# A fused adaLN, long-convolution and shift-mixer kernel: input rows turned on TensorE, two swap buffers exchanged, the half block of the third layer split over two column groups, and about ninety single moves in a written-out order

## The chip, the core and the metric

The kernel runs on one core of a Trainium2 chip. The core has a matrix engine (TensorE, PE in the profile, with PEld for its weight loads), a vector engine (VectorE, DVE), an activation engine (ScalarE, ACT), a general engine (GpSimd, POOL) and a queue engine (SyncE, SP) that issues most of the DMAs. The metric is device microseconds of one execution. Lower is better.

## What is computed

All inputs are bf16. The sequence has S = 2048 rows of D = 640 channels; the hidden layer of the mixer has F = 1728.

```python
mod = (silu(c) @ w_mod)          # six vectors of 640: sa, ca, ga, sb, cb, gb
h = layernorm(x) * (1 + ca) + sa                 # x is A_q
k_shift = 4-tap causal filter of k along S, taps shift_k
kv = k_shift * v
y = causal long convolution of kv with ssm_k along S, by FFT of length 4096, + kv * ssm_D
x = x + ga * (h * y)
h = layernorm(x) * (1 + cb) + sb
u = gelu(layernorm(h) @ w1)                      # 640 x 640
u's four channel quarters are shifted along S by +1, -1, +2, -2 rows
x1 = h + u @ w2                                  # 640 x 640
h2 = gelu(layernorm(x1) @ w3) @ w4               # 640 x 1728, 1728 x 640
x = x + gb * (x1 + h2)
```

F is 13.5 blocks of 128, so w3 has a last block of only 64 columns, called the half block here.

## The kernel before, in words

**How the work is recorded and ordered.** Every piece of work is recorded by `add` as a task: an engine or a choice of engines, a closure that issues the instructions, and its reads and writes. Nothing is scheduled at run time. `ORDER` (line 26) is one string that lists all 1046 tasks by number, with the letter of the engine that is to run each (P, A, D, G for POOL, S for SP) and, after a colon, the places of the PSUM buffers that it takes (four of two banks each, 0 to 3). `Planner.run` checks that the string respects the dependencies, and then issues the tasks in that order. Each engine executes its own tasks strictly in this order. The `cost`, `rate` and `port` numbers of a task have no effect on this order. SP and POOL both issue DMAs, each through a queue of its own.

**The front (lines 224 to 387).** SP loads ssm_D as one column per channel block (line 224, `Dcol`, 640 elements of two bytes), the five blocks of the filter `ssm_k` (line 228, into Ra, 512 KB each), the shift taps (line 229, `skT`), the vector c (`c_col`) and, by transposing DMAs (line 233), k and v with channels on partitions. Meanwhile the twiddle tables of the FFT are made. POOL writes integer ramps (lines 287 and 302); `angles` multiplies and masks them on DVE (lines 292 and 293); `angles_pool` does the same in floating point with a rounding constant (lines 306, 308, 310), on POOL or DVE; ACT takes the sine (lines 316 and 321). F1bd is the table of the first FFT stage, Gs (in RG) that of the second, E (EA, EB, line 370) and H (via RK, copied into RH at line 576) those of the inverse. Of Gs a third is a negation (line 348), and six DMA copies spread it over partitions (lines 353 and 354). Line 355 makes the diagonal weights `diagw` of the shift filter out of `skT`. Lines 380 to 386 make silu(c) on POOL.

**The transforms.** Line 444 adds D to the filter's first sample, so that the skip path costs nothing later; `to_slots` (line 394) transposes 32x32 blocks on DVE; `stage1` (line 407) and `stage2_half` (line 427) are the two FFT stages on TensorE, evicted from PSUM by `evac` on ACT (line 207) or DVE (line 209). Stage one of the filter writes T01; half h = 0 is its lower half. `k_shift` (lines 463, 468) makes kv, which goes the same way. `inverse1` (lines 613, 617, 628, 629) multiplies the two spectra for ten blocks: for each block the filter's spectrum, with its two partition halves swapped, is copied by DMA into one of four swap buffers `KSY` (block i uses buffer i mod 4), one half issued on SP and one on POOL. `inverse2` (line 661) gives y, 16 row tiles of 128 rows.

**The layers.** `ln1_stats` takes the statistics of the first layer norm of a row tile, on DVE (two bn_stats and an aggregate, lines 539 and 540) or on ACT (two activations with an accumulator, lines 547 and 548). `chain_a`, `chain_b` and `chain_c` take groups of one or two tiles (`CG`) through the gating and two layer norms. `ln_finish` makes a norm's scale: the mean steps of lines 702 to 707 on POOL or DVE, then lines 712 to 717 on POOL, after the sum of squares from ACT (line 729). `turn` transposes a tile, on TensorE for early groups (line 772) and by a transposing DMA on SP for later ones (line 765). `mm_w1` (lines 818, 828), `mm_w2` (line 873), `mm_w3` (line 907, gelu at line 911) and `mm_w4` (lines 937 and 928) are the four layers; `mm_w2` and after work on the groups `MG`: seven pairs and the single tiles 1 and 0, tile 0 last. The result is stored by SP (lines 969 and 987).

**The half block.** Before, `w3_sb` is padded: a POOL copy (line 1020) repeats the last 64 columns behind themselves, so that the last block has 128 columns and its output holds the same 64 hidden channels on both partition halves. In `mm_w4` function `half` (line 928) uses that: for a pair, tile 0 takes its half block from partitions 0 to 63 and tile 1 from partitions 64 to 127, side by side.

## Time and profile before

| | |
|---|---|
| Runs | 301.48 us median of three (300.99 to 302.75) |
| The profiled execution | span 298.7 us from the first to the last instruction; what the runs' time holds beyond the span is 2.8 us by the median |
| PE | busy 269.7 us, 3176 matmuls |
| DVE, ACT, POOL | busy 218.2, 208.3 and 104.8 us |
| Granted TensorE clock | mean 0.975 of full speed |
| From 0 to 105 us | PE 90.6, DVE 101.1, ACT 93.6 us busy |
| From 105 to 140 us | PE 26.7, DVE 30.7, ACT 31.5 us busy, clock 0.84 |
| From 140 to 294 us | PE 152.4, DVE 85.6, ACT 83.2 us busy |
| DMA | 35.76 MB in 58356 packets, 40032 of them under 512 bytes |

A row of the profile names the source line, the engine, the operation, and output and input by the program's names with buffer numbers left out, so ps_w is any of the layers' PSUM tiles and R any tile called R with a number. A timeline row gives start and duration in us. In square brackets stand the idle time of that engine just before and what released it. A busy PE is modelled from its pipelined matmuls and overlaps a little from row to row; the chain of what ended last shows how far apart they really are.

### The profile page before, as it was taken

The page shows a single profiled execution, that of the slowest core. Times are in us where ns is not written, and L with a number is a line of the kernel's source. Part 1 is how long each engine was busy: PE and PEld are TensorE (multiplying, and loading weights), DVE is VectorE, ACT ScalarE, POOL GpSimd, SP SyncE. Part 2 cuts the span into 40 slices and gives each one's busy share as a digit, 9 for nine tenths or more (in the row PEclk, how much of TensorE's full clock was granted, in tenths as well). Part 3 has the DMA queues.
Part 4 walks back from the last instruction along what each step waited for, and adds up shares of the span by engine and source line. Part 5 has one row for each costly group of instructions (what it writes and reads, how often), then busy time and mean ns, then how long its engine had stood idle before and what let it go on. Part 6 is the DMA issues. An engine that isn't in the chain of part 4 may idle for free.

```text
span 298.7 us, 7890 instructions
## 1 busy us (share of the span) xinstructions
PE 269.7 (90%) x3176; PEld 208.5 (70%) x3182; DVE 218.2 (73%) x438; ACT 208.3 (70%) x341; POOL 104.8 (35%) x237
## 2 busy tenths in 40 slices
PE   0999999999989766869999999999999999999993
PEld 0666755777878436648878677787788767887871
DVE  8998999999999998898759589886361544212442
ACT  4799989999999789979868775766854705431200
POOL 5864364453216591434275426120421321100000
PEclk9999999999999859799999999999999999999999
DMA  6999999898999920563700203223113030510112
GB/s 215 275 215 184 225 137 246 225 217 221 229 253 281 280 65 2 153 203 69 273 4 0 46 5 68 56 46 60 41 40 80 5 89 6 63 43 23 29 52 60
DMA packets 58356, 35.76 MB, mean 120 GB/s; under 512 B 40032, under 2 KB 55008, under 8 KB 58320
## 3 DMA queue, kind: packets, MB, share of 16 engines
q1 hardware_dynamic: 57136, 32.01, 46.3%
q0 software_dynamic: 1088, 3.21, 4.1%
q8 instruction: 25, 0.41, 0.6%
q14 instruction: 11, 0.09, 0.1%
q10 hardware_dynamic: 96, 0.04, 0.1%
HBM read 16.31 MB, written 2.62 MB: 63 GB/s over the span
## 4 chain that ended last, share of the span: by engine, by line
PE 51%; DVE 13%; ACT 11%; DMA 10%; POOL 6%; issue 5%; SPq 2%; DVEq 0%; POOLq 0%; ACTq 0%
PE ps_w L937 17%; PE ps_w L907 14%; ACT T L207 5%; DMA Ra<-in_A_q_dram 5%; PE ps_w L873 4%; PE ps_w L818 3%; PE ps_s L427 3%; ACT RG L729 3%; DVE Rb L617 3%; PE ps_ksh L463 2%; POOL lnv L715 2%; PE ps_s L407 2%; DMA RK<-R 2%; DVE R L756 2%; PE ps_mod L493 2%
## 5 line engine op out<-in xcount | busy, mean ns | idle before, releaser
L907 PE MATMUL ps_w<-R,T 128*128 128x256 bf16 (+1 forms) x630 | 63.8, 261 | 0.7 <-DMA R<-RH 0.7
L907 PEld LDWEIGHTS <-T 128*128 128x128 bf16 x630 | 55.5, 98 | 7.9 <-issue 2.0
L937 PE MATMUL ps_w<-T,R 128*128 128x320 bf16 x416 | 59.1, 299 | 0.0
L911 ACT ACTIVATE R<-ps_w 128x1024 bf16<-128x1024 f32 (+2 forms) x36 | 28.8, 827 | 41.9 <-PE ps_w L907 41.9
L937 PEld LDWEIGHTS <-R 128*128 128x128 bf16 x416 | 40.5, 98 | 15.2
L960 DVE TENSOR_TENSOR T<-ps_w,R 128x640 bf16<-128x640 f32 x15 | 12.3, 822 | 35.4 <-PE ps_w L928 18.1
L207 ACT CAST T<-ps_s 128x1024 bf16<-128x1024 f32 x32 | 30.4, 1029 | 3.2 <-PE ps_s L407 3.1
L207 ACT CAST R<-ps_s 128x960 bf16<-128x960 f32 (+1 forms) x35 | 30.8, 964 | 1.8 <-PE ps_s L427 1.6
L407 PE MATMUL ps_s<-F1bd,Rb 128*128 128x256 bf16 x160 | 23.3, 298 | 8.7 <-DVE Rb L394 8.1
L729 ACT ACTIVATE RG<-R 128x640 bf16<-128x640 bf16 x32 | 23.5, 734 | 9.9 <-DVE R L880 6.7
L407 PEld LDWEIGHTS <-Rb 128*128 128x128 bf16 x160 | 16.7, 107 | 14.7 <-DVE Rb L394 8.6
L873 PE MATMUL ps_w<-RG,R 128*128 128x320 bf16 x160 | 23.2, 299 | 2.1 <-ACT R L820 2.1
L715 POOL TENSOR_TENSOR lnv<-lnv,mhalf 128x2 f32<-128x2 f32 (+1 forms) x29 | 22.5, 775 | 2.3
L427 PE MATMUL ps_s<-T,RG 64*128 64x160 bf16 x512 | 21.2, 230 | 0.8 <-ACT R L207 0.6
L880 DVE SCALAR_TENSOR_TENSOR R<-ps_w,R 128x640 bf16<-128x640 f32 x16 | 12.9, 819 | 11.8 <-PE ps_w L873 11.6
L427 PEld LDWEIGHTS <-RG 64*128 64x128 bf16 x512 | 17.7, 94 | 5.1 <-issue 4.6
L818 PE MATMUL ps_w<-R,RG 128*128 128x256 bf16 (+1 forms) x200 | 20.0, 259 | 1.3 <-DMA R<-RK 0.6
L873 PEld LDWEIGHTS <-R 128*128 128x128 bf16 x160 | 15.4, 98 | 8.2 <-ACT R L820 2.4
L629 PE MATMUL ps_i<-EB,Rb 128*128 128x128 bf16 x160 | 19.0, 219 | 1.5 <-DVE Rb L617 1.4
L818 PEld LDWEIGHTS <-RG 128*128 128x128 bf16 x200 | 17.1, 102 | 3.5 <-issue 2.0
L628 PE MATMUL ps_i<-EA,Rb 128*128 128x128 bf16 x160 | 19.0, 219 | 0.4 <-ACT R L207 0.3
L714 POOL TENSOR_TENSOR lnv<-stat,lnv 128x2 f32<-128x2 f32 x19 | 4.0, 212 | 40.9 <-ACT RG L729 28.7
(178 smaller groups left out, 513.5 us busy)
## 6 DMA issues: line engine op xcount, KB each, us to landing
Ra<-in_A_ssm_k_dram SPq DMA_DIRECT2D x5, 512.0 KB, 5.7
R<-in_w_mod_dram SPq DMA_DIRECT2D x6, 400.0 KB, 6.0
out_dram<-RH SPq DMA_DIRECT2D x60, 40.0 KB, 1.6
T<-in_B_w_dram SPq DMA_DIRECT2D x5, 432.0 KB, 6.2
RH<-in_w_mod_dram SPq DMA_DIRECT2D x4, 400.0 KB, 4.4
Ra<-in_A_q_dram SPq DMA_DIRECT2D x4, 320.0 KB, 6.6
RK<-R SPq DMA_DIRECT2D x5, 256.0 KB, 4.5
RK<-R POOLq DMA_DIRECT2D x5, 256.0 KB, 5.3
```

The source lines that it names most:

```text
L207: nc.scalar.copy(dst, src(ps.tile))
L407: nc.tensor.matmul(psv[:, ml, :], lhsT=xL[:, s0:s0 + P], rhs=F1r, start=True, stop=True)
L427: nc.tensor.matmul(psv[:, g, j], lhsT=Gs[p, k, 64 - 64 * cc:192 - 64 * cc], rhs=T1h[h][p, cc * 32 + k], start=(cc == 0), stop=(cc == 1), t ...
L628: nc.tensor.matmul(psv[:, w, :], lhsT=Av[:, r_, :, g_], rhs=EAf, start=True, stop=False)
L629: nc.tensor.matmul(psv[:, w, :], lhsT=Bv[:, r_, :, g_], rhs=EBf, start=False, stop=True)
L715: nc.gpsimd.tensor_tensor(rs, rs, mhalf[:, 0:n], ALU.pow)
L729: add("ACT", 0.74, lambda e: nc.scalar.activation(junk, src, ACT.Square, scale=float(D) ** -0.5, accum_out=stat[:, li, 1, t:t + 1]), r=[sk ...
L818: nc.tensor.matmul(pt[:, fb, 0:cw], lhsT=w1_sb[:, b, 160 * fb:160 * fb + P], rhs=hT[:, b, 0:cw], start=(b == 0), stop=(b == ND - 1))
L873: nc.tensor.matmul(pt[:, hf, 0:320], lhsT=gsf[:, fb, c0:c0 + P], rhs=w2_sb[:, fb, 320 * hf:320 * hf + 320], start=(fb == 0), stop=(fb == 4))
L907: nc.tensor.matmul(pt[:, fl, 0:cw], lhsT=w3_sb[:, b, fb * P:(fb + 1) * P], rhs=xT[:, b, 0:cw], start=(b == 0), stop=(b == ND - 1))
L911: nc.scalar.activation(g3[g % 2][:, f0:f0 + fn, 0:cw], ps.tile[:, 0:fn, 0:cw], ACT.Gelu_apprx_tanh)
L937: nc.tensor.matmul(bank(i, hf), lhsT=gg[:, fb, i * P:(i + 1) * P], rhs=w4_sb[:, fb, 320 * hf:320 * hf + 320], start=(fb == 0 and i == 0), ...
```

## The change

Five things are changed, and the order string is new as a whole because the tasks have new numbers (1054 of them now).

- **Rows turned on TensorE.** ssm_D, c and shift_k are loaded as contiguous rows of five partitions into T01 (free until the first FFT stage writes it). A 5x5 identity `eye`, made by POOL, and one matmul (for D) and five matmuls (for c and the four taps) turn them into columns, which ACT copies out of PSUM into `Dcol` and `csk`. `diagw` is laid out tap first. In the order SP issues one block of ssm_k first, then the D row, two blocks, the rows of the taps and of c, then the last two blocks.
- **Table front.** An early sine on ACT of a constant comes first. The small per-partition constants are split: nine one-column steps stay on DVE, six go to POOL. The two multiplications of the first Gs table (line 292) go from DVE to ACT, and its negation from DVE to ACT. The second Gs table has its scaling for both offsets on POOL and the two steps after the second one on DVE, where they were on DVE and POOL, and its negation moves from POOL to DVE. All five additions of D are on DVE (three were on POOL). The six copies of Gs are issued by POOL instead of SP.
- **Swap buffers.** In `KSY` the third and fourth entries are exchanged: the third block now uses the end of Rb and the fourth the upper half of RK, which holds the H table until its copies into RH are done. The order of the two blocks' copies on SP and POOL is exchanged too.
- **Half block.** `mm_w3` computes the half block with ten matmuls, 64 weight columns by 128 rows each, on two column groups of the array: for a pair, tile 0 on output partitions 0 to 63 and tile 1 on 64 to 127; for a single tile the same tile on both. The gelu of a pair then reads 384 columns instead of 512 in that task. The POOL copy of line 1020 is gone, and `half` reads its operand at columns 0 to 127 for both halves.
- **Moves.** The order of the PE tasks stays but for nine that move by one to four places. On ACT and DVE about fifty tasks stand elsewhere or change sides: the statistics of row tiles 14 and 10 go from DVE to ACT, several normalisations and turned tiles change between the two, and the mean steps of `ln_finish` for tiles 7 and 8 (second norm) and 9 and 10 (first norm) go from POOL to DVE. On SP the transposing copy of the second tile of the mixer group of tiles 8 and 9 moves ahead of that of the first and of three stores, and a few stores swap places. 156 of 223 PSUM tasks have another place.

```diff
-    diagw = RQ[:, 0:2560].rearrange("p (b j m) -> p b j m", b=ND, j=4)
+    diagw = RQ[:, 0:2560].rearrange("p (j b m) -> p b j m", b=ND, j=4)
...
-    KSY = [(RG[:, 6144:8192], ("RG", 6144, 8192)), (RK[:, 0:2048], ("RK", 0, 2048)), (RK[:, 2048:4096], ("RK", 2048, 4096)), (Rb[:, 8192:10240], ("Rb", 8192, 10240))]
+    KSY = [(RG[:, 6144:8192], ("RG", 6144, 8192)), (RK[:, 0:2048], ("RK", 0, 2048)), (Rb[:, 8192:10240], ("Rb", 8192, 10240)), (RK[:, 2048:4096], ("RK", 2048, 4096))]
...
-
-    def ld_tiny(q, dst, src):
-        with nc.allow_non_contiguous_dma(reason="tiny"):
-            q.dma_start(dst, src)
-
-    dma("SP", 8, lambda q: ld_tiny(q, Dcol[:], A_ssm_D.rearrange("(b p) -> p b", p=P)), w=[("Dcol", 0, 1)], rate=8.0)
+    csk = mem.tile([P, 5 * ND], BF, name="csk")
+    c_col, skT = csk[:, 0:ND], csk[:, ND:5 * ND].rearrange("p (j b) -> p b j", j=4)
+    rowD, rowc, rows = T01[0:ND, 0:P], T01[0:ND, P:2 * P], T01[0:ND, 2 * P:6 * P]
+
+    dma("SP", 8, lambda q: q.dma_start(rowD, A_ssm_D.rearrange("(b p) -> b p", p=P)), w=[("T01", 0, P)])
...
-    dma("SP", 8, lambda q: q.dma_start(skT[:], A_shift_k.rearrange("(b p) j -> p b j", p=P)), w=[("skT", 0, 1)], rate=30.0)
-    dma("SP", 8, lambda q: ld_tiny(q, c_col[:], c.rearrange("o (b p) -> p (o b)", p=P)), w=[("ccol", 0, 1)], rate=12.0)
+    dma("SP", 8, lambda q: q.dma_start(rows, A_shift_k.rearrange("(b p) j -> b (p j)", p=P)), w=[("T01", 2 * P, 6 * P)])
+    dma("SP", 8, lambda q: q.dma_start(rowc, c.rearrange("o (b p) -> (o b) p", p=P)), w=[("T01", P, 2 * P)])
...
+    one, eye = T01[:, 6 * P + 16:6 * P + 17], T01[:, 6 * P:6 * P + ND]
...
+        nc.vector.memset(one, 1.0)
...
-    add("DVE", 0.35, f, w=[("consts", 0, 1), ("kTp", 0, 1)])
+    add("DVE", 0.35, f, w=[("consts", 0, 1), ("kTp", 0, 1), ("T01", 6 * P + 16, 6 * P + 17)])
...
+        nc.vector.tensor_single_scalar(pci[:, 1:2], pidx[:], 63, ALU.bitwise_and)
+        nc.vector.tensor_single_scalar(pci[:, 2:3], pidx[:], 64, ALU.bitwise_and)
...
-        nc.vector.tensor_single_scalar(pci[:, 1:2], pidx[:], 63, ALU.bitwise_and)
+        nc.vector.tensor_single_scalar(pci[:, 3:4], pidx[:], 96, ALU.bitwise_and)
+        nc.vector.tensor_copy(s64[:], pci[:, 1:2])
+        nc.vector.tensor_copy(offi[:], pci[:, 2:4])
...
-        nc.vector.tensor_scalar(s32o[:], pci[:, 0:1], 2.0, 1.0, ALU.mult, ALU.add)
-        nc.vector.tensor_copy(s64[:], pci[:, 1:2])
-        nc.vector.tensor_scalar_mul(s32o[:], s32o[:], 1.0 / 8192)
-        nc.vector.tensor_scalar_mul(s64t[:], s64[:], 1.0 / 8192)
-
-        nc.vector.tensor_single_scalar(pci[:, 0:1], pidx[:], 64, ALU.bitwise_and)
-        nc.vector.tensor_single_scalar(pci[:, 1:2], pidx[:], 96, ALU.bitwise_and)
-        nc.vector.tensor_copy(offi[:], pci[:])
...
-        nc.vector.tensor_scalar(offc[:, 2:3], offi[:, 0:1], s64t[:], 0.5, ALU.mult, ALU.mult)
-        nc.vector.tensor_scalar(offc[:, 4:5], offi[:, 1:2], s32o[:], 0.5, ALU.mult, ALU.mult)
...
-        nc.vector.tensor_scalar_add(offc[:, 3:4], offc[:, 2:3], 0.25)
-        nc.vector.tensor_scalar_add(offc[:, 5:6], offc[:, 4:5], 0.25)
-    add("DVE", 1.9, f, r=[("pidx", 0, 1)], w=[("scol", 0, 1)])
+    add("DVE", 1.3, f, r=[("pidx", 0, 1)], w=[("scol", 0, 1)])
+
+    def f(e):
+        nc.gpsimd.tensor_scalar(s64t[:], s64[:], 1.0 / 8192, None, ALU.mult)
+        nc.gpsimd.tensor_scalar(offc[:, 2:3], offi[:, 0:1], s64t[:], 0.5, ALU.mult, ALU.mult)
+        nc.gpsimd.tensor_scalar(offc[:, 3:4], offc[:, 2:3], 0.25, None, ALU.add)
+        nc.gpsimd.tensor_scalar(s32o[:], s32[:], 2.0 / 8192, 1.0 / 8192, ALU.mult, ALU.add)
+        nc.gpsimd.tensor_scalar(offc[:, 4:5], offi[:, 1:2], s32o[:], 0.5, ALU.mult, ALU.mult)
+        nc.gpsimd.tensor_scalar(offc[:, 5:6], offc[:, 4:5], 0.25, None, ALU.add)
+    add("POOL", 1.0, f, r=[("scol", 0, 1)], w=[("scolt", 0, 1)])
+
+    add("POOL", 0.2, lambda e: nc.gpsimd.affine_select(out=eye, in_=one.to_broadcast([P, ND]), pattern=[[-1, ND]],
+                                                       compare_op=ALU.is_equal, fill=0.0, base=0, channel_multiplier=1),
+        r=[("consts", 0, 1), ("T01", 6 * P + 16, 6 * P + 17)], w=[("T01", 6 * P, 6 * P + ND)])
+    psD, psC = Slot(), Slot()
+
+    def f(e):
+        pt = pst(psD, name="ps_row")
+        nc.tensor.matmul(pt[:, 0, 0:ND], lhsT=rowD, rhs=eye[0:ND, :], start=True, stop=True)
+    add("ACT", 0.1, lambda e: nc.scalar.activation(lnv[:, 2, 0:1], b_pos[:], ACT.Sin), r=[("consts", 0, 1)], w=[("lnsp", 0, 1)])
+    t0 = add("PE", 0.1, f, r=[("T01", 0, P), ("T01", 6 * P, 6 * P + ND)], alloc=psD, ni=2)
+    t1 = add("ACT", 0.2, lambda e: nc.scalar.copy(Dcol[:], psD.tile[:, 0, 0:ND]), w=[("Dcol", 0, 1)], use=psD)
+
+    def f(e):
+        pt = pst(psC, name="ps_row")
+        nc.tensor.matmul(pt[:, 0, 0:ND], lhsT=rowc, rhs=eye[0:ND, :], start=True, stop=True)
+        for j in range(4):
+            nc.tensor.matmul(pt[:, 0, ND + ND * j:2 * ND + ND * j], lhsT=rows.rearrange("b (p j) -> b j p", j=4)[:, j, :], rhs=eye[0:ND, :], start=True, stop=True)
+    t0 = add("PE", 0.5, f, r=[("T01", P, 6 * P), ("T01", 6 * P, 6 * P + ND)], alloc=psC, ni=10)
+    t1 = add("ACT", 0.2, lambda e: nc.scalar.copy(csk[:], psC.tile[:, 0, 0:5 * ND]), w=[("ccol", 0, 1), ("skT", 0, 1)], use=psC)
...
-    def angles(reg, o, n, pattern, base, s_col, q, offs=None):
+    def angles(reg, o, n, pattern, base, s_col, q, offs=None, split=False):
...
-                nc.vector.tensor_scalar(m_, ti, s_col, off, ALU.mult, ALU.add)
+                if not split:
+                    nc.vector.tensor_scalar(m_, ti, s_col, off, ALU.mult, ALU.add)
...
+            if split:
+                add("ACT", 0.25 + 0.00095 * n, lambda e, m_=m_, off=off: nc.scalar.activation(m_, ti, ACT.Identity, scale=s_col, bias=off),
+                    r=[keys[0], ("scol", 0, 1)], w=[k_])
...
-                r=[keys[0], ("scol", 0, 1)], w=[keys[1]], port=0.5)
+                r=[keys[0], ("scol", 0, 1), ("scolt", 0, 1)], w=[keys[1]], port=0.5)
...
-            ms, ma, ky = angles("R3", o, 512, pat, base, s64[:], 8192, (offc[:, 0:1], offc[:, 1:2]))
+            ms, ma, ky = angles("R3", o, 512, pat, base, s64[:], 8192, (offc[:, 0:1], offc[:, 1:2]), True)
...
-        add(("POOL", "DVE"), {"POOL": 1.48, "DVE": 0.35}, lambda e, k2s=k2s: eng_of[e].tensor_scalar(Gs[:, k2s, 128:192], Gs[:, k2s, 0:64], -1.0, None, ALU.mult),
-            r=[wk[:3]], w=[wk], port=0.4)
+        def f(e, k2s=k2s):
+            if e == "ACT":
+                nc.scalar.mul(Gs[:, k2s, 128:192], Gs[:, k2s, 0:64], -1.0)
+            else:
+                eng_of[e].tensor_scalar(Gs[:, k2s, 128:192], Gs[:, k2s, 0:64], -1.0, None, ALU.mult)
+        add(("POOL", "DVE", "ACT"), {"POOL": 1.48, "DVE": 0.35, "ACT": 0.65}, f, r=[wk[:3]], w=[wk], port=0.4)
...
-        in_=skT[:].rearrange("p b j -> p (b j)").unsqueeze(2).to_broadcast([P, 4 * ND, P]),
+        in_=csk[:, ND:5 * ND].unsqueeze(2).to_broadcast([P, 4 * ND, P]),
...
+                    if fb == NF - 1:
+                        for b in range(ND):
+                            for i in range(2):
+                                c0 = P * i if cw > P else 0
+                                nc.tensor.matmul(pt[64 * i:64 * i + 64, fl, 0:P], lhsT=w3_sb[:, b, fb * P:fb * P + 64], rhs=xT[:, b, c0:c0 + P],
+                                                 start=(b == 0), stop=(b == ND - 1), tile_position=(0, 64 * i))
+                        continue
...
-                nc.scalar.activation(g3[g % 2][:, f0:f0 + fn, 0:cw], ps.tile[:, 0:fn, 0:cw], ACT.Gelu_apprx_tanh)
+                if cw > P and f0 + fn == NF:
+                    n = cw * (fn - 1) + P
+                    gf = g3[g % 2].rearrange("p f n -> p (f n)")
+                    nc.scalar.activation(gf[:, f0 * cw:f0 * cw + n], ps.tile[:].rearrange("p f n -> p (f n)")[:, 0:n], ACT.Gelu_apprx_tanh)
+                else:
+                    nc.scalar.activation(g3[g % 2][:, f0:f0 + fn, 0:cw], ps.tile[:, 0:fn, 0:cw], ACT.Gelu_apprx_tanh)
...
-            nc.tensor.matmul(bank(i, hf), lhsT=gg[p, NF - 1, i * P:(i + 1) * P], rhs=w4_sb[p, NF - 1, 320 * hf:320 * hf + 320],
+            nc.tensor.matmul(bank(i, hf), lhsT=gg[p, NF - 1, 0:P], rhs=w4_sb[p, NF - 1, 320 * hf:320 * hf + 320],
...
-    def f(e):
-
-        nc.gpsimd.tensor_copy(w3_sb[:, :, F:FP], w3_sb[:, :, F - 64:F])
-    add("POOL", 0.6, f, w=[("T01", 0, ND * FP)])
...

```

## What I predict, before seeing a run of it

> **What bounds the kernel now.** I read first the ten-microsecond windows (columns: PE, weight loads, DVE, ACT, POOL busy us with instruction counts, granted clock, DMA share, GB/s), since the average (PE 90%, DVE 73%, ACT 70%) mixes stages.
>
> ```profile
> 0.00:10.00 10.00, 1.88 (x9) 1.35 (x10) 8.84 (x32) 3.96 (x6) 6.60 (x16) 1.00 0.74 249
> ...
> 70.00:80.00 10.00, 9.29 (x181) 8.44 (x180) 9.87 (x11) 9.98 (x13) 2.05 (x4) 1.00 0.93 230
> ...
> 110.00:120.00 10.00, 7.63 (x168) 6.41 (x169) 8.95 (x24) 9.07 (x19) 3.13 (x17) 0.84 0.01 2
> ...
> 130.00:140.00 10.00, 7.25 (x95) 6.07 (x95) 8.43 (x24) 8.54 (x18) 3.94 (x11) 1.00 0.32 80
> ...
> 220.00:230.00 10.00, 10.00 (x91) 8.66 (x89) 3.79 (x11) 3.91 (x9) 2.64 (x9) 1.00 0.19 39
> ```
>
> There are three stages. Up to about 105 us DVE and ACT are full (the transforms; PE only follows their evictions). From 105 to 140 a chain through DVE, ACT and POOL (the layer norms) sets the pace and PE waits. From 140 to 294 PE is full, so only TensorE time or a PE wait counts. Behind it lie 4 us of last stores.
>
> Second, the timeline of the start (start, duration, idle before and its releaser):
>
> ```profile
> 0.80 0.46 SPq L224 DMA_DIRECT2D Dcol<-in_A_ssm_D_dram  x1
> ...
> 1.32 1.92 SPq L228 DMA_DIRECT2D Ra<-in_A_ssm_k_dram  x4
> ...
> 5.54 0.44 POOL L444 TENSOR_TENSOR Ra<-Ra,Dcol 128x1 bf16<-128x1 bf16 x1 [1.82 <-DMA Ra<-in_A_ssm_k_dram]
> ...
> 6.01 3.96 DVE L394 STREAM_TRANSPOSE Rb<-Ra 128x1024 int32<-128x1024 int32 x2
> ...
> 8.12 6.95 PE L407 MATMUL ps_s<-F1bd,Rb 128*128 128x256 bf16 x36 [8.12 <-DVE Rb L394]
> ...
> 9.19 2.84 ACT L207 CAST T<-ps_s 128x1024 bf16<-128x1024 f32 x3 [1.89 <-PE ps_s L407]
> ```
>
> DVE waits for the first filter block, ACT for PE: ACT is idle 6.0 of its first 9.19 us. Third, the timelines of the middle and of PE, where PE waits:
>
> ```profile
> 128.77 0.88 DVE L539 BATCH_NORM_STATS2 ln_st<-Ra 128x6 f32<-128x320 bf16 x2
> ...
> 129.69 0.21 DVE L540 BATCH_NORM_AGGREGATE mv<-ln_st 128x2 f32<-128x12 f32 x1
> ...
> 131.82 1.53 PE L873 MATMUL ps_w<-RG,R 128*128 128x320 bf16 x10 [2.08 <-ACT R L820]
> ...
> 170.72 2.34 PE L818 MATMUL ps_w<-R,RG 128*128 128x256 bf16 x20 [0.60 <-DMA R<-RK]
> ...
> 206.59 3.65 PE L907 MATMUL ps_w<-R,T 128*128 128x256 bf16 x32 [0.65 <-DMA R<-RH]
> ```
>
> After 141 us these last two are the only PE waits left: 1.25 us.
>
> **The front.** Before, the load of D in 640 two-byte pieces is queued first: the DMA view of the first 6 us shows 1 GB/s from about 1.9 us and the full 400 only from 3.5, so the first block lands at 5.40. After, that block is issued first, at 0.80. First bytes came 1.15 us after the first issue, 512 KB at 400 GB/s are 1.3, and some 0.6 passed from the last byte to the landing: 3.85. The D row, issued 0.46 later, comes at about 4.3; a matmul (0.3, as L407's), a copy of 5 columns (estimate 0.25, just under the 0.265 of the 32x128 activation) and the add on DVE (0.17) put the first transpose at about 5.2 instead of 6.01: 0.8 earlier, and PE and ACT with it.
>
> DVE then carries more: two 512-column steps of the second angle set come from POOL (L306 on DVE took 0.57, so 1.14) and two more adds (0.34); one L306 (0.57) goes to POOL; one negation (0.74) goes to ACT and the other comes from POOL. Net +0.9, which eats its 0.8. What leaves DVE ahead of the transposes (two multiplies of 0.54 and about six one-column steps) only ends in waiting for D. ACT gains 0.8 at the start and its 0.52 wait for POOL (L310) at 17.8, and pays one 25-column copy (0.25): -1.1. The two multiplies (0.65 each, as L316), the negation and the D copy fit its 6 us of idle time; the sine table load (1.28) starts at 0.79 either way. In a stage in which both engines are full I take the mean of about 0 and -1.1: **-0.5**. Bounds: -1.6 (the other 1280 tiny pieces, for the shift kernel and c, no longer sit between the transposing loads, and DVE's 0.38 and 0.51 us waits near 26 and 29 us go as well) and +1.5 (below).
>
> Covers. The shift and c rows share T01 with the first stage, so its h=0 evictions and everything behind five row matmuls on PE wait for them. Behind three blocks they land near 1.95 + 3x1.3 + 0.6 = 6.5; PE gets there at about 8.1: cover 1.6. If they take the 6.6 us of the old shift load (issue 3.2, landing 9.8), PE, ACT and DVE lose about 1.6. The six RG copies leave SP, which then starts the loads behind them sooner, for POOL: 6x0.5 of POOL time, and two POOL waits for landings. A copy from POOL landed in 5.3 us against 4.5 from SP (RK<-R). Behind them on POOL stand E, the H angles and the silu chain, which ended at 47.6 and is used at 54.0: 6.4 us of cover. The second stage (25.79) has only about 1 us; with the negation at about 19.5 the first copies land near 26: 0 to +1.5. I take 0, as PE is not the bound there.
>
> **Exchanged swap buffers.** The third and fourth exchange trade RK's upper half for Rb. The chain passes through those copies (67.4 to 76.1), but DVE, which uses them, is busy 9.87 of 10 between 70 and 80 us: 0, bounds -0.5 and +0.5.
>
> **The half block.** Seven pair groups spend five 256-column matmuls on it: the chain has 70 in 7.64, so 109 ns each, 0.55 per group. Two single groups spend 5x61 ns = 0.30 (20 of 128 columns in 1.22). After, ten matmuls of 64 columns of weights by 128, two at a time. No row shows two column halves; the nearest two:
>
> ```profile
> 254.78 0.45 PE L928 MATMUL ps_w<-T,R 64*128 64x320 bf16 x4
> ...
> 113.39 1.21 PE L661 MATMUL ps_i<-T,RH 32*32 32x160 bf16 x96
> 113.39 1.00 PEld L661 LDWEIGHTS <-RH 32*32 32x32 bf16 x96
> ```
>
> At the 136 ns of a 320-column matmul (26 in 3.53) a column is 0.425 ns. L928 (two row halves) takes 0.38 in the chain: two rounds of 136 ns, and 0.11 for the change of shape. The trace thus gives 5x54 + 110 = 0.38: -0.17 x7, +0.08 x2. The skill speaks against it. "TensorE: Matmul & The Clock Gate" (Part 3, What overlaps and what doesn't) lets a weight load overlap running matmuls only in another row group, and here both halves use all rows; its section on LDWEIGHTS gives columns/1.2 ns, 53 for 64, and "TensorEngine Tiling (Array Packing)" (Restrictions and Gotchas) rules out the fast load with column tiling. In series that is 10x(53+56) + 110 = 1.2 us: an estimate from these pages, +0.65 x7 and +0.9 x2, +6.4. But L661 uses four column and four row groups and loads 32 columns every 10.4 ns, where the rule gives 27, and 24 matmuls of 68 ns (160 columns) on one row group alone would fill 1.6 us, not 1.21. Column groups do overlap here, so I take the trace: -1.2 + 0.2 = **-1.0**, ends -2.0 (no change of shape) and +6.4. ACT saves 128 columns per pair (0.1), beside a full PE: 0. The POOL copy that filled the padding (0.45 at 135.49) goes; PE was busy with L873 then: 0.
>
> **The moves.** (a) The statistics of row tile 14 (L539, L540: 1.1 us) leave DVE at 128.8, where the chain passes through them, for ACT (two passes, 1.9), and some normalisations change sides. DVE's chain shortens by 1.1; ACT, busy 8.5 of 10, pays part back: **-0.8**, ends -2 (the whole 2.08 wait at 131.8) and +1.4 (ACT's net added work between 110 and 140, if ACT becomes last there). (b) The statistics of tile 10 (1.1 us at 156.8) leave the DVE chain that ends in the wait at 170.7, but ACT gets 1.9 and one normalisation (0.9) just ahead of the sums that POOL awaits next, and has about 1.7 of slack there: **-0.3**, ends -0.6 and +1.0. The mean steps that go from POOL to DVE ended 1.1 us before those sums: 0. (c) Of the pair of transposing copies (L765) that PE awaits at 206.6 the second was issued at 203.88, behind three stores (1.5 us on SP), and now goes ahead of them; it then lands by about 205, and PE comes at 205.9: **-0.6**, ends -0.65 and 0, and the stores have time. The other moves swap neighbours on engines with room: 0, ends -0.5 and +0.5.
>
> **Sum.** -0.5 - 1.0 - 0.8 - 0.3 - 0.6 = -3.2 on a span of 298.7, so 295.5. The median of the runs, 301.48, is 2.8 above the profiled span, taken as constant: **298.3**.
>
> **Rivals.** *Nothing but the half block*: the front ends in the same DVE work, and the middle is bound by ACT, which gets 1.4 us more. For: DVE's net +0.9, ACT above 9 of 10 from 110 to 130. Against: its 6 idle us at the start. 301.48 - 1.0 = 300.5; chance 0.17. *The front is worth more*: DMA is saturated from 4 to 34 us and 1920 tiny pieces go; the end -1.6, all of the 2.08 and 1.25 us waits, and -1.0: 301.5 - 5.9 = 295.6; chance 0.17. *Column halves run in series* (the slower side): 6.4 us on the full PE against 2.2 of gains elsewhere, 305.7. It passes +1.5 when the ten matmuls take over 0.9 us: nine groups then cost 8.1 against 4.4 before, +3.7 less the 2.2. L661 speaks against it; with smaller such losses (late rows, a stage-two stall) chance 0.11. The forecast itself, 296.5 to 299.9: 0.55.
>
> A measurement of this kernel can tell about 0.5%, 1.5 us, from no change. Faster 0.55 + 0.17 = 0.72, same 0.17, slower 0.11. The range leaves out the top (column halves in series) and a little below: 294.8 to 301.8.
>
> **What would show it.** First transpose near 5.2 and first eviction near 8.4; no PE wait at the five row matmuls; PE beginning its full stretch about 1.3 us earlier; ten L907 half matmuls within about 0.4 us; no waits at the two copies. It would be wrong if the halves take over 0.55 us, if stage two waits for RG, or if ACT is what PE awaits near 130.

## The result and the profile after

The changed kernel takes **306.22 us** (median of 14 runs, 302.32 to 307.80) against 301.81 (300.62 to 304.91) for the kernel before on the same chip: ratio **1.0112 [1.0088, 1.0136]**. This ratio, like all ratios with an interval here, leaves out runs over 1.5% above their kernel's own fastest; since kernels with copies on POOL spread widely, the ratio of the plain medians (here 1.0146) is given too. The forecast was 298.3 with a range up to 301.8, so it was wrong in sign. The profiled execution has a span of 304.1 (before 298.7) and itself took 305.98.

The windows of after, with the columns of the prediction's first fence:

```profile
0.00:10.00 10.00, 2.61 (x16) 1.60 (x17) 7.41 (x25) 6.52 (x13) 8.60 (x22) 1.00 0.75 257
10.00:20.00 10.00, 7.57 (x36) 4.54 (x35) 9.54 (x10) 7.12 (x8) 4.69 (x5) 1.00 1.16 222
...
30.00:40.00 10.00, 8.56 (x173) 6.51 (x175) 7.60 (x8) 7.65 (x9) 6.71 (x11) 1.00 1.28 195
...
70.00:80.00 10.00, 9.64 (x187) 8.03 (x187) 9.77 (x12) 9.78 (x13) 4.22 (x9) 1.00 0.86 232
...
110.00:120.00 10.00, 6.40 (x125) 3.88 (x124) 9.55 (x28) 8.97 (x19) 7.68 (x22) 0.53 0.27 61
...
130.00:140.00 10.00, 8.31 (x58) 5.74 (x59) 8.29 (x25) 9.33 (x21) 4.94 (x11) 0.83 0.64 211
...
220.00:230.00 10.00, 10.00 (x91) 7.57 (x90) 6.40 (x16) 5.11 (x10) 2.66 (x9) 1.00 0.18 39
```

The early windows are the ones to read. ACT is busy 6.52 of the first ten (before 3.96), as foretold. But from 30 to 40 DVE and ACT are down to 7.60 and 7.65, where before they had 9.50 and 9.49: in the stage in which both should be full, both wait. The DMA share is above 1 from 10 to 50 us. Before, in this window, and a mark that both kernels have, the first matmul into ps_mod, in before and in after:

```profile
30.00:40.00 10.00, 9.63 (x181) 7.02 (x177) 9.50 (x13) 9.49 (x12) 2.70 (x2) 1.00 1.17 207
...
54.04 0.84 PE L493 MATMUL ps_mod<-RH,silu_w 128*128 128x320 bf16 x5
...
59.70 0.84 PE L527 MATMUL ps_mod<-RH,silu_w 128*128 128x320 bf16 x5
```

The mark comes 5.7 us late, which is as much as the whole loss (span +5.4). By PE's rows the loss is complete even earlier: the eight stage-one matmuls that begin at 41.35 in before begin at 46.94 in after. What follows gives a little back.

The timeline of the start of after (start, duration, idle before and its releaser) answers the second fence:

```profile
4.79 2.07 DVE L428 STREAM_TRANSPOSE Rb<-Ra 128x1024 int32<-128x1024 int32 x1
...
6.91 1.89 PE L441 MATMUL ps_s<-F1bd,Rb 128*128 128x256 bf16 x8 [2.56 <-DVE Rb L428]
...
7.98 1.02 ACT L208 CAST T<-ps_s 128x1024 bf16<-128x1024 f32 x1 [1.25 <-PE ps_s L441]
...
9.46 0.18 PE L300 MATMUL ps_row<-T 5*128 5x5 bf16 x1 [0.67 <-DMA T<-in_c_dram]
...
10.37 3.23 DVE L478 TENSOR_TENSOR Ra<-Ra,Dcol 128x1 bf16<-128x1 bf16 x1 [0.36 <-DMA Ra<-in_A_ssm_k_dram]
...
10.37 2.48 POOL L389 TENSOR_SCALAR_AFFINE_SELECT RQ<-csk 128x2560 bf16<-128x2560 bf16 x1
12.84 0.75 POOL L336 TENSOR_SCALAR R<-R,s64t,offc 128x512 f32<-128x512 int32 x1
```

The first transpose stands at 4.79 (before 6.01), the first eviction at 7.98 (9.19): 1.2 us early. At 10.37 that lead is lost and more: an addition of one column, 0.17 elsewhere, takes 3.23 us on DVE. It starts with one POOL instruction and ends as the next one ends (12.84 + 0.75 = 13.59). This is the loudest row of the page. The PE waits of after are the second suspect:

```profile
30.51 1.69 PE L461 MATMUL ps_s<-T,RG 64*128 64x160 bf16 x43 [1.10 <-DMA RG<-RG]
...
37.97 3.63 PE L461 MATMUL ps_s<-T,RG 64*128 64x160 bf16 x87 [0.65 <-DMA RG<-RG]
...
138.47 1.53 PE L906 MATMUL ps_w<-RG,R 128*128 128x320 bf16 x10 [1.35 <-ACT R L853]
...
147.55 0.72 PE L861 MATMUL ps_w1x<-R,RG 128*128 128x256 bf16 x5 [1.19 <-DMA R<-RK]
```

Stage two now waits for the Gs copies. Before, in this stretch, its starts waited for evictions:

```profile
25.79 1.83 PE L427 MATMUL ps_s<-T,RG 64*128 64x160 bf16 x44 [0.16 <-ACT T L207]
...
31.98 4.03 PE L427 MATMUL ps_s<-T,RG 64*128 64x160 bf16 x96 [0.21 <-ACT R L207]
```

The wait before the 320-column matmuls is 1.35 instead of 2.08, those at 170.7 and 206.6 are gone, and one for a copy stands at 147.55.

### The profile page after: what moved, and what is told of

It is laid out like the page before. It is cut to its first block, busy times and chain, and to the rows that moved or that the text cites. A ratio compares the mean times of both kernels' runs of the same rounds, so it can differ in the third digit from the quotient of the medians.

```text
span 304.1 us, 8017 instructions
## 1 busy us (share of the span) xinstructions
PE 273.5 (90%) x3233; PEld 208.0 (68%) x3233; DVE 219.0 (72%) x434; ACT 214.9 (71%) x355; POOL 105.0 (35%) x242
## 4 chain that ended last, share of the span: by engine, by line
PE 58%; ACT 13%; DMA 12%; DVE 9%; issue 4%; SPq 1%; POOL 1%; DVEq 0%; ACTq 0%; POOLq 0%
PE ps_w L982 17%; PE ps_w L947 15%; PE ps_w L906 7%; DMA RG<-RG 5%; PE ps_w L851 4%; ACT R L208 3%; ACT T L208 3%; PE ps_s L441 3%; DMA R<-RK 3%; PE ps_s L461 3%; ACT RG L762 2%; PE ps_ksh L497 2%; DMA Ra<-in_A_ssm_k_dram 2%; DMA RG<-in_B_w_dram 2%; DVE Rb L650 2%
## 5 line engine op out<-in xcount | busy, mean ns | idle before, releaser
L947 PE MATMUL ps_w<-R,T 128*128 128x256 bf16 (+1 forms) x585 | 60.8, 261 | 0.0
L947 PEld LDWEIGHTS <-T 128*128 128x128 bf16 x585 | 51.2, 98 | 7.3 <-issue 1.1
L956 ACT ACTIVATE R<-ps_w 128x1024 bf16<-128x1024 f32 (+2 forms) x29 | 25.2, 886 | 31.9 <-PE ps_w L947 27.5
L208 ACT CAST T<-ps_s 128x1024 bf16<-128x1024 f32 x32 | 30.8, 1020 | 5.8 <-PE ps_s L441 5.6
L441 PE MATMUL ps_s<-F1bd,Rb 128*128 128x256 bf16 x160 | 24.7, 305 | 5.5 <-DVE Rb L428 5.0
L906 PE MATMUL ps_w<-RG,R 128*128 128x320 bf16 x160 | 24.6, 310 | 1.3 <-ACT R L853 1.3
L748 POOL TENSOR_TENSOR lnv<-lnv,mhalf 128x2 f32<-128x2 f32 (+1 forms) x29 | 21.2, 733 | 2.3
L497 PE MATMUL ps_ksh<-R,RQ 128*128 128x512 bf16 x80 | 19.0, 381 | 0.0
```

The costliest lines, as they stand in the source:

```text
L208: nc.scalar.copy(dst, src(ps.tile))
L441: nc.tensor.matmul(psv[:, ml, :], lhsT=xL[:, s0:s0 + P], rhs=F1r, start=True, stop=True)
L497: nc.tensor.matmul(pt[:, i, :], lhsT=diagw[:, b, jj, :], rhs=kT[:, b, c0:c0 + 512], start=(jj == 0), stop=(jj == 3))
L748: nc.gpsimd.tensor_tensor(rs, rs, mhalf[:, 0:n], ALU.pow)
L906: nc.tensor.matmul(pt[:, hf, 0:320], lhsT=gsf[:, fb, c0:c0 + P], rhs=w2_sb[:, fb, 320 * hf:320 * hf + 320], start=(fb == 0), stop=(fb == 4))
L947: nc.tensor.matmul(pt[:, fl, 0:cw], lhsT=w3_sb[:, b, fb * P:(fb + 1) * P], rhs=xT[:, b, 0:cw], start=(b == 0), stop=(b == ND - 1))
```

## The experiments

All are edits of the two kernels. Ratios are to the kernel before, run beside it on the same chip; "of medians" is the ratio of the plain medians. Only e5 is beyond 2%.

| kernel | median us | of medians | ratio [95%] |
|---|---|---|---|
| after | 306.22 | 1.0146 | 1.0112 [1.0088, 1.0136] |
| e1: addition on POOL | 307.13 | 1.0148 | 1.0084 [1.0055, 1.0112] |
| e2: Gs copies on SP | 302.15 | 0.9983 | 0.9984 [0.9964, 1.0004] |
| e3: both | 301.89 | 0.9975 | 0.9979 [0.9960, 0.9998] |
| e10: e2, scalar addition | 302.07 | 0.9977 | 0.9983 [0.9964, 1.0001] |
| e5: before, Gs copies on POOL | 311.93 | 1.0316 | 1.0280 [1.0228, 1.0332] |
| e8: e3, third copies on POOL | 305.66 | 1.0108 | 0.9995 [0.9962, 1.0027] |
| e9: e3, third copies on ACT | 304.17 | 1.0059 | 1.0036 [1.0010, 1.0061] |
| e16: e8, v ahead of x | 304.13 | 1.0061 | 1.0075 [1.0052, 1.0097] |
| e17: e8, x waits for copies | 305.13 | 1.0094 | 1.0059 [1.0029, 1.0090] |
| e4: before, half block | 302.52 | 0.9995 | 0.9993 [0.9971, 1.0015] |
| e6: after, but front of before | 300.40 | 0.9935 | 0.9929 [0.9906, 0.9951] |
| e12: e6 without half block | 300.06 | 0.9910 | 0.9912 [0.9880, 0.9944] |
| e7: e4, repaired front of after | 303.91 | 1.0038 | 1.0048 [1.0028, 1.0068] |
| e11: e6, v ahead of x | 301.45 | 0.9956 | 0.9950 [0.9932, 0.9968] |
| e13: e6 and 14 PE instructions | 301.41 | 0.9978 | 0.9971 [0.9947, 0.9994] |
| e14: e3, shift task earlier | 302.73 | 1.0022 | 1.0024 [1.0004, 1.0044] |
| e15: e3 and 49 PE instructions | 301.53 | 0.9982 | 0.9970 [0.9950, 0.9991] |

### Which of the two suspects: the addition or the Gs copies

Edits of the order string of after: e1 the first pair of lines, e2 the others, e3 all. On before, e5 sends the same six copies to POOL.

```diff
-75D
+75G
...
-42G 43G 44G 55G 56G 57G
+42S 55S 56S 43S 44S 57S
```

> The changed kernel with one letter of the order changed: the one-column addition of D for filter block 0, which took 3.23 us on DVE at 10.37 while POOL ran the diagonal weights (2.48) and an angle step (0.75), runs on POOL just ahead of them. Theory (the stall is DVE waiting for something that POOL holds): no one-column addition over 0.3 us, the transpose of block 0 starts near 10.9 instead of 13.64, PE's wait of 2.43 at 15.73 goes, the last modulation matmuls come 2 to 3 us earlier, and the ratio to the kernel before falls from 1.011 to between 1.001 and 1.004. Rival (the front is limited by the loads and their landing, the stall only sits in time that would be idle): 0 to 0.7 us, ratio 1.009 to 1.011.

> The changed kernel with the six copies of Gs back on SP, in SP's old sequence. Theory (the copies on POOL's queue land after 5 to 7 us instead of 3.7, and POOL waits in its queue for them): no PE wait for RG in the second stage (1.10 and 0.65 before it), the EA and EB scalings of POOL start before 27 instead of 31.56, and the ratio falls from 1.011 to between 1.004 and 1.008; the 3.2 us stall of the addition stays. Rival (second stage is late only since everything ahead of it is late): ratio 1.010 to 1.012.

> Both edits together. Theory (they are the whole loss of the front): the modulation matmuls end within 0.5 us of the kernel before, and with the half block the ratio is 0.994 to 0.998. Rival (the row loads, or the moves in the middle, carry the rest of the loss): ratio 1.001 or more, with PE's waits for the rows or for ACT near 130 left.

> The kernel before with one thing changed: the six copies of Gs are issued by POOL instead of SP, at the same places of the order. Theory (these copies on POOL's queue are the loss by themselves): the copies of the third part (line 354) land after 6 to 10 us instead of 4.8, PE waits 1 to 4 us for RG in the second stage, ratio 1.010 to 1.017. Rival (they cost only because the changed front makes the second table late): PE waits under 0.5 us, ratio under 1.004.

The copies decide. Putting them back on SP takes the medians from 1.0148 to 0.9975 (e1 to e3) and from 1.0146 to 0.9983 (after to e2): 1.7 and 1.6 points, 5.2 and 4.9 us. By the ratios with intervals it is 1.05 and 1.28 points, 3.2 and 3.9 us. The copies on POOL alone make before 2.8% slower. The loud row is not what the time hangs on: with the copies on POOL, taking the 3.23 us addition off DVE left the loss within the intervals (1.0112 and 1.0084) and the mark in ps_mod at 59.7; with them on SP it is worth 0.05 to 0.08 points (e2 to e3), less than the intervals can tell. The expectation for e1 fell with it.

Where the copies cost is seen in e1. The timeline of PE:

```profile
36.33 5.28 PE L461 MATMUL ps_s<-T,RG 64*128 64x160 bf16 x87 [3.96 <-DMA RG<-RG]
```

The wait is paid for twice here, as the window of e1 from 34 to 40 us shows:

```profile
34.00:40.00 6.00, 3.67 (x56) 3.67 (x58) 1.94 (x2) 1.93 (x2) 0.00 (x0) 0.50 1.23 145
```

The granted clock stands at 0.50, and the 87 matmuls behind the wait take 5.28 us, where after, at 1.00, ran them in 3.63. The clock falls so between 30 and 49 us in the profiles of e1, e5, e8, e16 and e17 alone. In after's own profile it does not.

Each table has three copies: two, and a third (L388, in before L354) that reads what they wrote. In before the first pair lands in 3.2 to 3.9 us, the third in 4.6 to 5.0. On POOL the first pair takes 3.2 to 7.2 and the third 6.9 to 8.2 (after), or 6.2 and 10.5 (e1). The two stand in series, and POOL stands in between: in e1 it waits 5.22 us ahead of the second table's third copy (issued at 25.74), in after 6.75, in e5 7.91. In e5 that also holds DVE, by the timelines of POOL and of DVE:

```profile
29.78 1.03 POOL L354 DMA_DIRECT2D RG<-RG  x2 [7.91 <-DMA RG<-RG]
30.81 0.62 POOL L302 IOTA RK<- 128x512 int32 x1
...
31.47 0.61 DVE L306 TENSOR_SCALAR RK<-RK,s32o,offc 128x512 f32<-128x512 int32 x1 [7.24 <-POOL RK L302]
```

The iota that DVE needs is queued on POOL behind the issue that waits for a landing: 7.24 us of DVE, in a kernel that loses 9.5 by medians. In after that iota (L332, at 13.57) is ahead of the copies that wait, so after does not have this wait.

### Why copies from POOL land late

On e3, the third copies alone go to POOL (e8) or to ACT (e9); e16 and e17 then change what SP queues beside them.

```diff
-44S 57S
+44G 57G
```

```diff
-        return add(eng, {"SP": 0.5, "POOL": 0.6}, lambda e: fn(nc.sync if e == "SP" else nc.gpsimd), r, w, kb=kb, rate=rate, lat=lat)
+        return add(eng, {"SP": 0.5, "POOL": 0.6, "ACT": 0.6}, lambda e: fn({"SP": nc.sync, "ACT": nc.scalar, "POOL": nc.gpsimd}[e]), r, w, kb=kb, rate=rate, lat=lat)
...
-44S 57S
+44A 57A
```

> The kernel with both edits of the front (additions and Gs copies put right), but the third copy of each Gs table (line 388, two transfers of 192 KB) is issued by POOL, at the place where SP would issue it. Theory (a transfer from POOL's queue lands late while SP's loads keep the transfer engines full): landing after 6 to 10 us instead of 4.8, PE waits 1 to 4 us for RG, ratio 1.003 to 1.012. Rival (what costs is that POOL issues the third copies only after it has waited for the first ones): landing and ratio as with SP, 0.996 to 1.000.

> As the kernel with the third copies on POOL, but ACT issues these two transfers at the same place. If the kind of POOL's queue makes them late, they land in about 4 to 5.5 us here and the ratio is within 0.003 of that with SP (0.998). If what counts is only that they no longer stand in SP's queue ahead of the later loads, they land in 6 to 10 us here too, and the ratio is that of the run on POOL, 1.003 to 1.012.

The landing is 4.8 us from SP (e3), 5.9 to 6.2 from ACT, 7.7 to 9.1 from POOL. By medians e8 loses 1.3 points against e3 and e9 0.8. But e8's runs spread from 300.5 to 308.4, and its ratio with interval (0.9995) shows no loss. Its profile, in which PE waits 1.52 and 1.49 us for these copies, is of a run of 306.48; what a run near 301 does was not profiled. So e8 shows the late landing, and a loss in about half of its runs.

The DMA view of e1, first from 26 to 32 us and then from 32 to 36.3 (queue, packets, MB, share of the engines), tells what becomes of the copy issued at 25.74:

```profile
q1 hardware_dynamic: 1459, 1.27, 135.0%
...
q1 hardware_dynamic: 1005, 0.26, 72.4%
q0 software_dynamic: 48, 0.20, 25.5%
```

q0 is POOL's queue. For six us not one of its packets runs, while q1, the queue of SP, moves 1.27 MB, mostly the four loads of x (4 x 320 KB). SP issued them at 22.95, ahead of the copy, since it no longer had the copies in its own order; in e3 they are issued at 26.24, behind them. So the copy is less slow than late to start. The loads are not all of it, though: from 31.9 to 32.9 us the engines move only 0.02 MB, with nearly all of the copy still to move. Two runs test the order:

```diff
+                        q.dma_start(probe[64:128, 8 * kb:8 * kb + 8], RG[64:128, 1536 * kb:1536 * kb + 8])
...
-193S 63A
+13S 193S 63A
```

The first line is e17 (SP reads a little of what both third copies wrote before it issues x), the others e16.

> The kernel with both repairs and the third copies on POOL (e8), and on SP the load of v's next block issued ahead of the four loads of x. If the third copies come late because SP has already queued the 1.28 MB of x ahead of them, they now meet a load of another kind and their landing falls from 8.4 us to 6 or less, PE's two waits of 1.5 us for them shrink below 0.5, and the span falls from 304.6 to about 302. If POOL's way of issuing makes them late whatever stands in the queues, they land in about 8 us again and the span stays at 304.

> The same kernel (e8), but SP first issues two tiny copies that read what the third copies wrote, so the loads of x start only when those have landed. If the copies were late because of the loads ahead of them, they now land in 5 us or less and PE does not wait for them; the loads of x and v come some 5 us later instead, and DVE's wait for v (about 1 us) grows by 3 to 5. If POOL's way of issuing makes them late, the landing stays near 8 us though nothing new is queued beside them, and PE waits for them as in e8.

Both landings fall, to 5.4 to 5.8 (e16) and 5.3 to 5.4 (e17), and PE no longer waits for the copies. The precedence of x made most of the delay in e8; POOL's own part is about 0.6 us (5.4 against e3's 4.8; each is one profile). The expected time did not come. In e16 PE stands 1.96 us ahead of a k_shift task near 40 us (below), and in e17 what was pushed back is late: DVE waits 2.40 us for x and 1.18 for v and PE 3.22 behind them. With DMA full from 10 to 40 us, a place in the queue is the scarce thing, and the copies need the one they had on SP.

"DMA: Bandwidth & Descriptors" of the Trainium skill (section Queues, rings and completion order) says that each engine takes turns between queues, packet by packet. An estimate from it: with half of the 211 GB/s, 192 KB pass in 1.9 us. In after the two queues do share from 28 to 30 us (59 and 61% against 41 and 49%), but in e1 there was no sharing for 6 us. The trace decides. Why the copy got no turn there stays open; that the engines were nearly idle in the last of these microseconds speaks for something late on POOL's side.

### The addition

e10 is e2 with `Dcol` in f32 and the additions written as `tensor_scalar`, so that only one operand is a tensor.

```diff
-    Dcol = mem.tile([P, ND], BF, name="Dcol")
+    Dcol = mem.tile([P, ND], F32, name="Dcol")
...
-eng_of[e].tensor_tensor(sT[:, b, 0:1], sT[:, b, 0:1], Dcol[:, b:b + 1], ALU.add)
+eng_of[e].tensor_scalar(sT[:, b, 0:1], sT[:, b, 0:1], Dcol[:, b:b + 1], None, ALU.add)
```

> The changed kernel with the Gs copies on SP (in which the addition for block 0 took 2.19 us on DVE beside POOL's diagonal weights), but each addition of D takes the D value as a per-partition scalar in f32 instead of a second tensor operand. Theory (DVE waits because an operation with two operands in SBUF needs what POOL holds): 0.2 us or less for each of the five, the transpose of block 0 near 10.9, ratio 0.996 to 0.999. Rival (any small DVE operation waits there, or it is a late landing that only looks like a long addition): still 2 us or more beside POOL's row, ratio 0.998 to 1.000.

The timelines of DVE and POOL in e10:

```profile
9.81 0.22 DVE L478 TENSOR_SCALAR Ra<-Ra,Dcol 128x1 bf16<-128x1 bf16 x1 [0.51 <-DMA Ra<-in_A_ssm_k_dram]
...
9.57 2.47 POOL L389 TENSOR_SCALAR_AFFINE_SELECT RQ<-csk 128x2560 bf16<-128x2560 bf16 x1
```

Beside the same POOL instruction the addition now takes 0.22; in e2, as `tensor_tensor`, it took 2.19 (10.61 to 12.80, POOL 10.31 to 12.78). For this addition the number of tensor operands decides whether DVE is held, and yet the time stays where e2 had it. It is not the whole rule: before has a negation with one tensor operand that takes 0.74 on DVE while POOL runs L310, where the same takes 0.24 to 0.27 in e3 and after.

```profile
9.18 1.28 POOL L310 TENSOR_TENSOR R<-R 128x512 f32<-128x512 f32 x1
...
9.87 0.74 DVE L348 TENSOR_SCALAR RG<-RG 128x512 bf16<-128x512 bf16 x1
```

### The half block and the moves

e4 is before with the new `mm_w3`, its order otherwise kept. e6 takes the order, swap buffers and half block of after, but the first 236 tasks of before; e12 is e6 with the old `mm_w3`.

```diff
+                                nc.tensor.matmul(pt[64 * i:64 * i + 64, fl, 0:P], lhsT=w3_sb[:, b, fb * P:fb * P + 64], rhs=xT[:, b, c0:c0 + P],
+                                                 start=(b == 0), stop=(b == ND - 1), tile_position=(0, 64 * i))
```

> The kernel before with the half block alone: ten 64-column matmuls on two column groups, the gelu of 384 columns, no padding copy; the order otherwise the same. Theory: 0.40 us for ten matmuls where five took 0.55, so 0.8 to 1.1 us less, ratio 0.996 to 0.998. Rival (column halves in series): ratio over 1.005.

> The kernel before up to its 236th task (the whole front), and from there on the changed kernel's order, with exchanged swap buffers and the half block. Theory (the moves behind the front do little, and the half block saves about nothing since 0.10 us are lost ahead of it): ratio 0.996 to 1.000. Rival (the moves between 97 and 148 us cost the 1 us that the two traces differ by there): ratio 1.002 to 1.005. Second rival (the prediction: 2.7 us gained by moves and half block): ratio 0.990 to 0.993.

> The run without the front, with the half block as before (five 256-column matmuls and the padding copy), so the moves and the exchanged swap buffers alone. Theory (the half block saves nothing in sum: 0.05 us in each of seven pair groups less 0.2 in each of the two single ones; the moves take away 2.0 us of PE waits): ratio 0.992 to 0.995, as with the half block. Rival (the half block's 1 us shows once the waits are gone): 0.996 to 0.998.

The half block gives nothing: e4 is at 0.9993, and e6 with it no faster than e12 without. The timeline of PE in e4:

```profile
207.60 0.71 PE L914 MATMUL ps_w<-R,T 128*128 128x256 bf16 x5 [0.22 <-DMA R<-RH]
208.24 0.47 PE L910 MATMUL ps_w<-R,T 128*64 128x128 bf16 x10
208.64 4.54 PE L914 MATMUL ps_w<-R,T 128*128 128x256 bf16 x40
213.02 3.69 PE L949 MATMUL ps_w<-T,R 128*128 128x320 bf16 x26
```

Read the starts. The ten half matmuls take 208.64 - 208.24 = 0.40, as forecast; column groups do run at once. But the five whole ones ahead take 0.64 instead of 5 x 0.109 = 0.545: 0.10 us are lost where the shape changes. The group is 5.42 from first to last start; before's 50 took 5.45 (206.59 to 212.04). That is 0.03 to 0.05 gained on each of seven pairs, and the two single tiles lose 0.23 each (65 and 10 in 4.30, 70 in 4.07): about nothing.

The moves and the swap buffers are worth 0.64 points (e4 to e6, 1.9 us) or 0.88 (e12 alone, 2.7 us). e12, at 0.9912 [0.9880, 0.9944] from 7 runs, and e6 cannot be told apart; both beat both kernels.

### The front without its faults

e7 is the other corner of the square: after's front with both repairs, on e4.

> The changed kernel's front with the two repairs (the addition for block 0 on POOL, the copies of Gs on SP), then the kernel before's order and swap buffers, with the half block: the fourth corner of the square front by rest. Theory (the front ends where v's transposing loads land, near 40 us, so that starting 1.2 us earlier brings nothing): as the half block alone, ratio 0.997 to 1.001. Rival 1 (the repaired front still costs 1.5 us, as the difference of the run with both repairs to the run without the front says): 1.003 to 1.006. Rival 2 (the prediction, front 0.5 to 0.8 us better): 0.994 to 0.997.

| ratio | order of before | order of after |
|---|---|---|
| front of before, half block | 0.9993 (e4) | 0.9929 (e6) |
| repaired front, half block | 1.0048 (e7) | 0.9979 (e3) |

The repaired front costs 0.50 to 0.55 points, 1.5 to 1.7 us, with either order, though its first transposes are early. Four runs looked for the reason. Of their theories only a number came true, e13's ratio, and not for the reason given:

> The run without the front (0.993), in which DVE waited 1.3 us near 40 us for a transposing load of v; here that load is issued ahead of the four loads of x (1.28 MB) instead of behind them, and the two statistics that read x first move behind the next kv products on DVE. Theory (the front is bound by when v lands): DVE's wait for v goes, the modulation matmuls come 0.7 to 1.5 us earlier, ratio 0.988 to 0.992. Rival (DVE and ACT are full there anyway, or DVE waits for x instead): within 0.002 of 0.993 or above it.

> The run without the front (old front, new rest, ratio 0.993), with seven extra 4-column matmuls on PE, 14 instructions, at its first use near 8 us, which write a PSUM place that is overwritten at once; everything else is the same. Theory (PE stands where its program passes about the 705th instruction, until a block of instructions arrives behind v's load): the stand moves from inside the k_shift task of block 2 to its start, near 38.9, lasts until 40 to 41, 1.2 to 2 us, and the ratio rises by 0.3 to 0.5 points, to 0.996 to 0.998. Rival (PE waits for data or a buffer, and the front's rows or tables cost the 1.5 us): no stand there, ratio 0.992 to 0.994.

> The kernel with both repairs (ratio 0.998), with one PE task moved: the second k_shift task of block 2 goes ahead of two second-stage tasks (24 matmuls) instead of behind them. Theory: PE runs both k_shift tasks near 35.7 to 39.9 and the second-stage tasks up to the 705th instruction before it has to stand, the block has come by then, the stand is under 0.6 us, ratio 0.993 to 0.996. Rival (a wait for data in that task): PE waits as long ahead of it as before, now from 37.6, ratio 0.998 or more.

> The kernel with both repairs, with 25 extra 4-column matmuls on PE near 6.5 us (49 instructions more, as one event instruction goes). Theory: the place falls at the end of the first k_shift task of block 2, so PE stands from about 37.5 until near 40, 2 to 3 us instead of 1.5, and two second-stage tasks and ACT's evictions of them come after it; ratio 1.000 to 1.004 (0.998 before). Rival: the stand stays ahead of the second k_shift task with 1.5 us, ratio as before plus at most 0.002 for the extra work.

```diff
-184S 181S 183S 182S 13S
+13S 184S 181S 183S 182S
...
+                        nc.tensor.matmul(psv[:, 0, 0:4], lhsT=xL[:, s0:s0 + P], rhs=F1r[:, 0:4], start=True, stop=True)
...
-148P:0 152P:3 149A 197D 133P:1
+133P:1 148P:0 152P:3 149A 197D
```

These are e11 (the statistics of x moved behind too), e13 (e15 has 25 of the same kind with other weights; what they write is overwritten) and e14. All fronts come to about 40 us and then wait for the load of v (DVE: 1.03 in e3, 1.34 in e6), so an early start has nothing to run on; but v ahead of x (e11) did not help. The other trail was a stand of PE (a stop for which the profile shows no cause) near 40 us, by the timeline of e3 and then of e13:

```profile
40.05 1.90 PE L497 MATMUL ps_ksh<-R,RQ 128*128 128x512 bf16 x8 [1.51 <-ACT RK L346]
```

```profile
39.26 0.23 PE L432 MATMUL ps_s<-T,RG 64*128 64x160 bf16 x1 [0.31 <-issue]
```

In e3 the event that the task needs, ACT's eviction of its PSUM buffer, had come at 38.0, two us before PE went on; the row names a later one. In e6 PE stands inside the same task (0.49, after six of its eight matmuls), and with 14 instructions more (e13) one matmul ahead of it: the stand stays at about the 705th PE instruction. The traces show what may end it. A queue of the kind "instruction" (q8) brings single packets of 16 KB. One of them ends at 38.74 in e3, at 39.50 in e6 and at 37.97 in e13, and PE goes on 1.3 to 1.4 us later. In all seven profiles with a stand the distance is 1.3 to 1.5, and in the other twelve PE comes to this place no sooner after the packet. So PE seems to wait there for a block of its program; the times fit, but no edit tested it. The time does not follow this stand: e13 stands 0.31 and e15 not at all, and both are at 0.997.

What the repaired front loses against e6 stands elsewhere in the profiles. By the mark in ps_mod e3 is no later than e6 (55.4 and 55.2), nor at the first 320-column matmuls (127.04 and 127.09). It loses at one later place, by the timelines of PE in e3, e6 and e13:

```profile
143.09 0.71 PE L861 MATMUL ps_w1x<-R,RG 128*128 128x256 bf16 x5 [1.49 <-DMA R<-RK]
...
142.27 0.71 PE L828 MATMUL ps_w1x<-R,RG 128*128 128x256 bf16 x5
...
142.89 0.71 PE L833 MATMUL ps_w1x<-R,RG 128*128 128x256 bf16 x5 [1.33 <-ACT RG L552]
```

PE waits there for a turned tile, a transposing copy on SP. In e3 15 of the copy's 16 landing signals come by 141.14 and the last at 142.96; in e13 it is 141.14 and 142.76 (its row names another event), in e6 all 16 are there by 141.79. This wait, 0.8 to 1.6 us, is in all twelve profiles with the front of after and in e13, and in none of the other six. So the loss goes with the number of PE instructions ahead and not with the rows or the tables: the old front with 14 more of them (e13) has the same wait and loses 0.42 of the 0.50 points. In each of the 13 a 16 KB instruction packet runs while the copy is under way (140.88 to 141.76 in e3); but one also ran in e6 and e11, whose copies were not late. That the packet delays the copy is therefore likely and not shown. In e7 the wait is 0.84, half of what e7 loses against e4, and in e15, with 49 instructions more, it is 0.81; the rest of the loss stays open.

## Why the prediction was wrong

It wanted -3.2 us; the medians say +4.4, the ratio with interval +3.4. The difference of 7.6 us (6.6) by the prediction's own steps:

- **"The second stage (25.79) has only about 1 us ... 0 to +1.5. I take 0, as PE is not the bound there": the step that failed, 4.9 us (3.9 by the ratio with interval).** The suspicion was right (it is on the list of what would make the forecast wrong) and its price was not. "A copy from POOL landed in 5.3 us against 4.5 from SP" was taken from a later copy; at 20 to 40 us, with the DMA share above 1, the third copies took 6.2 to 10.5 (after and e1). Only the first copies were counted ("the first copies land near 26"), but the third of each table follows them, so two late landings stand in series, with a wait in POOL's queue between. And "SP, which then starts the loads behind them sooner" was written down as a fact without a price: those loads went ahead of the copies (e1), and with other loads there the copies landed 2 to 4 us sooner (e8 against e16 and e17). That PE is not the bound there excuses nothing, since DVE and ACT live on what PE gives them.
- **The front, "-0.5": it is +1.5 with both faults repaired** (2.0 us). The early start was underestimated (first transpose 4.79, forecast 5.2; first eviction 7.98, forecast 8.4), but what leads at 8 us is gone by 40. The rows' cover of 1.6 us did not hold in after, where PE waited 0.67 for c's row (in e3 it did not wait). The sum had no term for a wait behind the front: by e3 and e13 most of the +1.5 is the wait near 143 us (in e7 half of it), which comes with the added PE instructions.
- **"Two more adds (0.34)": one of them took 3.23**, and its repair moved the time by nothing that the intervals can tell. Before's own profile had a sign that DVE can be held beside POOL, the negation of 0.74; I priced it as its duration. The section Who interferes with whom of "SBUF — State Buffer" in the Trainium skill has a rule for the addition (a DVE instruction with two inputs in SBUF against a POOL instruction that reads SBUF); e10's 0.22 against 2.19 agrees with it.
- **The half block, "-1.0": nothing** (1.0 us). The skill's objection (in series, 1.2 us) was rightly set aside: the ten take 0.40, so the rival of +6.4 is out. The mis-sized term is "0.11 for the change of shape": there is one more at the entry, 0.10 per group (0.64 against 0.545 in e4). "TensorEngine Tiling (Array Packing)" of the Trainium skill (Key Properties) says, without a figure, that changing the tiling mode drains PE; the 0.10 agrees.
- **The moves, "-0.8", "-0.3" and "-0.6": right in their sum** (-1.7; measured -1.9 and -2.7 with the swap buffers). The waits at 170.7 and 206.6 went as told. The 2.08 became 1.31 in e6, but it was 1.35 in e4 without the moves too, so the share of (a) alone is not shown.

The rivals priced a slower outcome by one mechanism, column halves, which did not happen; the true one was inside "a stage-two stall", in one clause of it.

## What to carry to other kernels

When a transfer changes its queue, price three things where DMA is full: the landing in that very stage, each landing in series with it, and what the old queue now issues ahead of it. A wait that is moved to an engine's queue is paid by whatever stands behind it, as e5's iota. The loudest stall of a profile need not be what the time hangs on: repair it alone and see. And before a loss of half a per cent is put down to what a new stage does, add as many small instructions, of no use to the result, to the old one: here 14 of them brought most of the loss (e13).

## What was not expected of the hardware

- A copy of 192 KB issued by POOL moved no byte for 6 us beside 1.27 MB of SP's loads, where 28 to 30 us in after shows both queues sharing.
- After, e1, e5 and e8, with copies on POOL, spread over 4.7 to 8.6 us from run to run, and e9, with copies on ACT, over 5.7; the other kernels over 2.0 to 5.0.
- PE stands 0.3 to 2.0 us at its 701st to 705th instruction, wherever that falls in the work, and goes on 1.3 to 1.5 us after a 16 KB packet of an instruction queue has ended (seven profiles).
- 14 small PE instructions near 8 us brought a wait of 1.33 us near 143 us, for a copy whose last landing signal came 1.6 us after the other 15 (e13 against e6).
